# Global attention's value products: hi and lo parts side by side, 5 matmuls in place of 13

## The chip, the cores and the metric

One core of a Trainium2 chip runs the whole program. The metric is device time in microseconds (us) of one execution of the program, the median of several runs. The engines named here are TensorE (PE; PEld is its weight load), VectorE (DVE), ScalarE (ACT), GpSimd (POOL) and SyncE (SP, which issues the DMAs).

## The reference

The program computes attention and, on its output, a two-layer network without gating.

```python
# batch 8, heads 8, 512 local and 32 global positions, head size 64; window 32
k_all = concat([k_g, k_l]);  v_all = concat([v_g, v_l])
out_g = softmax(q_g @ k_all.T / 8) @ v_all                 # 32 global queries see all 544 keys
out_l = softmax([q_l @ k_g.T / 8, banded(q_l @ k_l.T / 8)]) @ concat([v_g, v_l])
x = concat([out_g, out_l]).transpose(0, 2, 1, 3).reshape(8 * 544, 512)
h = maximum(x @ w_in, 0)                                    # w_in 512 x 2048
y = (h * h) @ w_out                                         # w_out 2048 x 512
```

The change lies in the product of `out_g`: probabilities of the global queries times all values.

## The kernel before

**Split numbers.** Most products are made in a rounded fp32 form (F32R). A number is kept as a head (the value rounded to that form, by a copy on ACT) and a rest (value minus head, by a subtraction on DVE), and a product becomes head x head + head x rest + rest x head: three matmuls that add up in one PSUM tile.

**Steps.** A loop over t runs one step for each piece of local attention (16 half sequences of 256 queries, times 8 heads: t = 0 to 127), and in the same step one eighth of a block of the network (step m = t - 9 of it). Within a step PE does, in this order: the transposes of the last piece's probabilities (`pt`), the scores of this piece (`s`), the first layer (`h`, 24 matmuls in two halves), the last piece's value product (`xa`), a part of the global scores (`gs`), and the second layer for the network's step before (`o`, 12 matmuls). ACT and DVE prepare what these need: the row maximum (DVE; CUSTOM_DVE_ANT_0 in the profile, ISA in the lists below), `exp` (ACT, `prob`), the heads `ph` (four ACT copies) and rests (`pl`, `ph`) of the probabilities, the relu `r` of `h` and its square (on ACT in the steps where t mod 16 is in `SQ`, 2, 3, 4, 5, 14 or 15, else on DVE), the head `x_h` and rest `x_l` of the attention output, and in `split_head(t + 1)` the head `hi` (ACT) and rests `lo` and `hi` (DVE) of the queries, keys and values of the next piece, which the next step's scores read.

**Order.** From t = 17 on, PE, DVE and ACT issue their instructions in the order of the code (`FREE`, `keep_in_program_order`); before that a scheduler may reorder them. An instruction that waits holds back all that is behind it on its engine. In a step, the head and rest of the network's `r` (`act2`: `gh` on ACT, `gl` on DVE) come ahead of the jobs of place 1, the last of the step.

**Global attention.** Four heads of a batch (a group) form one global softmax; there are 16 such groups, and each needs two value products, one per pair of heads (`g_av`, pair 0 and pair 1). The jobs of a group are hung into steps by the table at line 654: with d mod 16 = 11 or 1, the probabilities are transposed at the end of step d + 2 (`g_tr`), their rests are made in step d + 3 (`g_rest`), `g_av` of pair 0 stands at the very end of step d + 3 (t mod 16 = 14 or 4), and `g_av` of pair 1 at the end of step d + 6 (t mod 16 = 1 or 7). One step later `g_x` transposes the result `gxs` into `xg` (DVE). `g_av` (line 333) makes 13 matmuls with 64 weight columns and 128 moving columns into one tile `gxo`: for each of four chunks of keys head x head, head x rest and rest x head, and one more for the last 32 keys, whose head and rest already share their partitions. Then ACT scales `gxo` by the reciprocal of the softmax's sum into `gxs`. `gxo` shares its PSUM buffer with `xa` (tag "xa").

**Output.** In every step with t mod 8 = 2, `evac` copies two finished tiles of the network's output to SBUF (ACT, `ot`).

Of the kernel before, what the change touches and what calls it, by code (L numbers as in the profile page):

```python
# [7 lines left out]
F32 = mybir.dt.float32  # L8
F32R = mybir.dt.float32r
I32 = mybir.dt.int32  # L10
AF = mybir.ActivationFunctionType
# [5 lines left out]
P = 128  # L17
# [20 lines left out]
def f(ap):  # L38
    return ap.bitcast(F32)
# [19 lines left out]
def attention_moe(  # L59
# [10 lines left out]
    pe, ve, ac = InOrder(tc, nc.tensor), InOrder(tc, nc.vector), InOrder(tc, nc.scalar)  # L70
# [3 lines left out]
    p2 = ctx.enter_context(tc.tile_pool(name="p2", bufs=2))  # L74
    p1 = ctx.enter_context(tc.tile_pool(name="p1", bufs=1))
    ps_h = ctx.enter_context(tc.tile_pool(name="ps_h", bufs=2, space=PSUM))
    ps_o = ctx.enter_context(tc.tile_pool(name="ps_o", bufs=1, space=PSUM))
    ps_a = ctx.enter_context(tc.tile_pool(name="ps_a", bufs=1, space=PSUM))
# [3 lines left out]
    def plain(t):  # L82
        return t < NPLAIN
# [179 lines left out]
    state = {}  # L263

    def g_load(t):

        b, grp = t // 16, (t // 4) % 2

        def cols(z, j):
            return bass.AP(z.tensor, z.offset + 64 * j, [list(z.ap[0]), [256, 2], [160, 2], [1, 32]])  # L270

        src = qg[b, grp].rearrange("p (a b) n -> p a b n", a=2)
        if plain(t):
            qz = p1.tile([P, 512], F32, tag=("ph", "gvl", "gvh", "ph")[t // 4], name=f"qz{t}")
            nc.gpsimd.memset(qz, 0.0)
            qr = p1.tile([P, 2, 2, 32], F32, tag="qr", name=f"qr{t}")
            (nc.sync if t else nc.scalar).dma_start(qr, src)
            nc.gpsimd.tensor_copy(cols(qz, 0), qr)
        else:
            qz = qgz  # L280
            qr = p1.tile([P, 2, 2, 32], F32, tag="qr", name=f"qr{t}")
            nc.sync.dma_start(qr, src)
            ac.copy(cols(qgz, 0), qr)
            ve.tensor_sub(cols(qgz, 1), qr, f(cols(qgz, 0)))
        state["qz"] = qz
# [32 lines left out]
    def g_split_v(t, pair):  # L318

        gv = state["gv"]  # L320
        gvh = p1.tile([P, 5, P], F32R, tag="gvh", name=f"gvh{t}_{pair}")
        gvl = p1.tile([P, 4, P], F32R, tag="gvl", name=f"gvl{t}_{pair}")
        ac.copy(gvh, gv)
        ve.tensor_sub(gvl, gv[:, :4, :], f(gvh[:, :4, :]))
        ve.tensor_sub(gvh[32:64, 4, :], gv[32:64, 4, :], f(gvh[32:64, 4, :]))
        state["gvs"] = gvh, gvl

    def g_soft(t):
        s = sg[:, (t // 4) % 2, :]
# [17 lines left out]
    def g_tr(t):  # L347

        s = sg[:, (t // 4) % 2, :]
        gt = ps_a.tile([P, 512], F32, tag="xa", name=f"gt{t}")  # L350
        for c in range(4):
            pe.transpose(gt[:, 128 * c : 128 * c + 128], s[:, 128 * c : 128 * c + 128], ident)
        pth = p1.tile([P, 640], F32R, tag="pth", name=f"pth{t}")
        ac.copy(pth[:, :512], gt)
        state["gpt"] = pth, gt

    def g_tr_last(t):

# [4 lines left out]
        state["ge"] = ge  # L363

    def g_rest(t):
        (pth, gt), ge = state["gpt"], state["ge"]
        ptl = p1.tile([P, 512], F32R, tag="ptl", name=f"ptl{t}")
        ac.copy(pth[:64, 512:], ge[:64, :])
        ve.tensor_sub(ptl, gt, f(pth[:, :512]))
        ve.tensor_sub(pth[64:, 512:], ge[64:, :], f(pth[:64, 512:]))  # L370
        state["gpt"] = pth, ptl

    def g_av(t, pair):
        (gvh, gvl), (pth, ptl) = state["gvs"], state["gpt"]
        xo = ps_a.tile([64, P], F32, tag="xa", name=f"gxo{t}_{pair}")
        mm = []
        for c in range(4):
            cols = slice(128 * c + 64 * pair, 128 * c + 64 * pair + 64)
            mm += [(pth[:, cols], gvh[:, c, :]), (pth[:, cols], gvl[:, c, :]), (ptl[:, cols], gvh[:, c, :])]
        mm.append((pth[:, 512 + 64 * pair : 576 + 64 * pair], gvh[:, 4, :]))  # L380
        for i, (x, y) in enumerate(mm):
            pe.matmul(xo, x, y, start=i == 0, stop=i == len(mm) - 1)
        xs = p1.tile([64, P], F32, tag="xs", name=f"gxs{t}_{pair}")
        ac.activation(out=xs, in_=xo, func=AF.Copy, scale=state["gst", t][:64, pair : pair + 1])
        state["xs"] = xs

    def g_x(t, pair):
# [114 lines left out]

    def evac(blk, tiles=(0, 1)):
        for i in tiles:
            pool, tag = ((p1, "ot"), (p2, "gl"))[i]
            ot = pool.tile([P, DM], F32, tag=tag, name=f"ot{blk}_{i}")
            ac.copy(ot, moe["o"][i])
            if blk < NGR:
                b, hf = divmod(blk, 2)
                r0 = b * 544 + 32 + hf * 256 + i * P  # L510
                nc.sync.dma_start(out[r0 : r0 + P, :], ot)
            else:
                for bb in range(4):
                    r0 = (4 * i + bb) * 544
                    nc.sync.dma_start(out[r0 : r0 + 32, :], ot[32 * bb : 32 * bb + 32, :])
# [59 lines left out]
    def w_done(m):  # L575
        w_used.update(range(4 * m, 4 * m + 4))
        for i in (4 * m, 4 * m + 2):
            w_free(i)

    g_load(0)  # L580
    for t in range(4, 8):
        load_head(t)
# [6 lines left out]
    for t in range(NSTEP + LAG + 1):  # L589
# [29 lines left out]
        if 0 < m <= NSTEP and m % 8 == 1 and m > 8:  # L619
            evac(m // 8 - 1)  # L620
# [24 lines left out]
        if live:  # L645
            if t % 2 == 1:
                g_evac(t)
            if t % 4 == 3 and t + 1 < NT:
                g_load(t + 1)
        elif t == NT:  # L650
            state["gs"] = None
        if live and t % 4 == 3 and (t // 8) % 2 == 1:
            d = t if t % 8 == 3 else t + 2
            for at, *job in (
                (d, 2, g_load_v, 0),
                (d + 1, 3, g_soft),
                (d + 1, 1, g_exp),
                (d + 2, 3, g_norm),
                (d + 2, 1, g_tr),
                (d + 3, 5, g_tr_last),  # L660
                (d + 3, 4, g_rest),
                (d + 3, 3, g_split_v, 0),
                (d + 3, 2, g_load_v, 1),
                (d + 3, 1, g_av, 0),
                (max(d + 4, 17), 3, g_x, 0),
                (d + 5, 2, g_split_v, 1),
                (max(d + 6, 17), 1, g_av, 1),
                (max(d + 7, 18), 3, g_x, 1),
            ):
                place, job, *args = job  # L670
                jobs.setdefault((at, place), []).append((job, t, *args))
        for job, *args in jobs.pop((t, 2), ()):
            job(*args)
        if m == NSTEP:
            for i in range(2):
                gemm2(m - 1, 0, (i,))
                gemm2(m - 1, 1, (i,))
                evac(NBLK - 1, (i,))
        elif m > 0:
            gemm2(m - 1, 0)  # L680
# [12 lines left out]
        if 8 * NGR - 2 <= m < 8 * NGR:  # L693
            cols = (slice(0, 224), slice(224, HALF))[m % 2]
# [76 lines left out]
```

## Time and profile before

| | |
|---|---|
| median of three runs | 1068.76 us (1068.66 to 1069.08) |
| the profiled execution | 1068.82 us, span 1067.0 us |
| granted TensorE clock | 1.0 throughout |
| busy | PE 98%, PEld 88%, DVE 80%, ACT 71% |
| matmuls | 7568, of them 416 of `g_av` |
| `g_av` | 32 of them, ACT's scaling 364 ns each |

In the timelines a row gives the start, the duration, the engine, the line, the operation, output<-inputs with the shape, how many rows are merged, and in brackets how long the engine sat idle before it and what it waited for. Line 52 is the helper that records every operation, so the tile names tell the place. Matmul durations overlap: the distance between two starts is what a matmul takes from the engine. A step of PE lasts from one `pt` to the next. The profiled execution ran 1.8 us beyond its span.

### The profile page before, as it was taken

To read this page: it belongs to the slowest core of one execution; us is meant where nothing else is said; L and a number is where in the kernel's file an instruction comes from. 1 tells how busy PE (TensorE), PEld (TensorE's weight loads), DVE (VectorE), ACT (ScalarE), POOL (GpSimd) and SP (SyncE) were. 2 spreads that over 40 slices of the span, in tenths; PEclk is the share of its full clock that TensorE was granted. 3 is DMA by queue.
4 is the path that set the end of the run, shared out by engine and by line. 5 is a ranking of instruction groups with operands and counts; after the bars stand their busy time and mean duration, and the time that the engine had idled before them with its cause. 6 is when DMAs were issued, how large, how long until landed. Compare 5 with 4: busy or idle time off the path is not lost.

```text
span 1067.0 us, 21142 instructions
## 1 busy us (share of the span) xinstructions
PE 1050.4 (98%) x7568; PEld 941.7 (88%) x7568; DVE 856.3 (80%) x2687; ACT 753.1 (71%) x1901; POOL 3.9 (0%) x14
## 2 busy tenths in 40 slices
PE   7999999999999999999999999999999999999998
PEld 6776889999998989998999989999999989999896
DVE  5698988898888989988888888888888888874321
ACT  5898877778777776778777777777777787774322
POOL 1000000000000000000000000000000000000000
PEclk9999999999999999999999999999999999999999
DMA  9772132223222322222322222223221322201000
GB/s 372 310 263 74 57 106 76 71 80 98 68 89 64 103 65 83 74 91 77 94 71 82 86 72 76 90 66 100 78 89 55 94 86 66 88 29 33 13 20 20
DMA packets 54312, 96.78 MB, mean 91 GB/s; under 512 B 4288, under 2 KB 29376, under 8 KB 54208
## 3 DMA queue, kind: packets, MB, share of 16 engines
q1 hardware_dynamic: 54064, 95.37, 27.2%
q8 instruction: 60, 0.98, 0.4%
q14 instruction: 44, 0.36, 0.1%
q10 hardware_dynamic: 144, 0.07, 0.0%
HBM read 86.51 MB, written 8.91 MB: 89 GB/s over the span
## 4 chain that ended last, share of the span: by engine, by line
PE 87%; ACT 7%; DVE 4%; issue 1%; DMA 0%; ACTq 0%
PE o L52 33%; PE h L52 32%; PE xa L52 7%; PE s L52 6%; PE pt L52 5%; PE gxo L52 2%; PE gs L52 2%; ACT prob L52 1%; DVE prob L52 1%; ACT r L52 1%; ACT ph L52 1%; ACT hi L52 1%; ACT ot L52 1%; PE gt L52 1%; ACT sg L52 0%
## 5 line engine op out<-in xcount | busy, mean ns | idle before, releaser
L52 PE MATMUL h<-x_h,ws 128*128 128x256 f32 x2048 | 388.9, 283 | 0.0
L52 PEld LDWEIGHTS h<-x_h,ws 128*128 128x128 f32 x2048 | 327.0, 191 | 0.5
L52 PE MATMUL o<-ws,gh 128*128 128x512 f32 x1024 | 321.3, 395 | 0.0
L52 PE MATMUL h<-x_l,ws 128*128 128x256 f32 x1024 | 289.1, 282 | 0.1
L52 PEld LDWEIGHTS o<-ws,gh 128*128 128x128 f32 x1024 | 185.5, 188 | 34.6
L52 PE MATMUL o<-ws,gl 128*128 128x512 f32 x512 | 202.6, 396 | 0.0
L52 PEld LDWEIGHTS h<-x_l,ws 128*128 128x128 f32 x1024 | 195.9, 191 | 0.9 <-DVE x_l L52 0.4
L52 ACT CAST ph<-pt 128x256 fp32r<-128x256 f32 x448 | 141.1, 341 | 67.7 <-PE pt L52 60.8
L52 ACT ACTIVATE prob<-prob,st 128x224 f32<-128x224 f32 x270 | 127.8, 475 | 61.2 <-DVE st L52 59.1
L52 ACT ACTIVATE r<-h 128x512 f32<-128x512 f32 x136 | 81.4, 599 | 112.3 <-PE h L52 112.3
L52 PEld LDWEIGHTS o<-ws,gl 128*128 128x128 f32 x512 | 96.2, 188 | 22.7
L52 DVE CUSTOM_DVE_ANT_0 prob<-s,con 128x224 f32<-128x224 f32 x256 | 90.0, 386 | 24.5 <-PE s L52 23.2
L52 DVE TENSOR_TENSOR gl<-r,gh 128x512 fp32r<-128x512 f32 x128 | 87.9, 686 | 23.3 <-ACT gh L52 20.5
L52 ACT CAST hi<-raw 128x864 fp32r<-128x864 f32 x112 | 102.5, 915 | 1.4
L52 DVE TENSOR_TENSOR r<-h,r 128x512 f32<-128x512 f32 x82 | 56.7, 692 | 51.9 <-ACT r L52 50.6
L52 PE MATMUL xa<-ph,hi 128*64 128x128 f32 x448 | 87.3, 238 | 1.6 <-DVE ph L52 1.2
L52 DVE TENSOR_TENSOR hi<-raw,hi 64x352 fp32r<-64x352 f32 x224 | 82.5, 368 | 6.4
L52 ACT CAST gh<-r 128x512 fp32r<-128x512 f32 x128 | 79.1, 618 | 9.1 <-DVE r L52 8.7
L52 DVE TENSOR_TENSOR ph<-pt,ph 64x128 fp32r<-64x128 f32 x224 | 79.6, 355 | 7.0
L52 DVE TENSOR_TENSOR lo<-raw,hi 128x448 fp32r<-128x448 f32 x112 | 69.6, 622 | 15.3 <-ACT hi L52 12.5
L52 PE MATMUL pt<-con,prob 128*128 128x128 f32 (+1 forms) x512 | 78.2, 274 | 0.7 <-ACT prob L52 0.5
L52 DVE TENSOR_SCALAR prob<-prob,st 128x224 f32<-128x224 f32 x242 | 70.7, 334 | 4.1
(80 smaller groups left out, 1572.7 us busy)
## 6 DMA issues: line engine op xcount, KB each, us to landing
raw<-in_pk_dram SPq DMA_DIRECT2D x127, 432.0 KB, 3.2
wr<-in_w_dram SPq DMA_DIRECT2D x32, 512.0 KB, 7.9
gv<-in_vg_dram SPq DMA_DIRECT2D x32, 320.0 KB, 3.3
out_dram<-ot SPq DMA_DIRECT2D x32, 256.0 KB, 2.2
qr<-in_qg_dram SPq DMA_DIRECT2D x31, 64.0 KB, 2.8
out_dram<-ot SPq DMA_DIRECT2D x8, 64.0 KB, 1.7
con<-in_consts_dram SPq DMA_DIRECT2D x2, 224.0 KB, 5.1
raw<-in_pk_dram SPq DMA_DIRECT2D x1, 304.0 KB, 3.2
```

The lines of the kernel that those rows point to most:

```text
L52: r = method(*args, **kwargs)
```

## The change

The heads and rests of the transposed probabilities go into one tile `pts`, interleaved so that 64 columns of heads and the 64 columns of their rests stand side by side for each chunk and pair. The heads and rests of the values go into one tile `gvs` of nine rows. A chunk is then one matmul with 128 weight columns (heads, rests) and 256 moving columns (value heads, value rests), into a PSUM tile of 128 partitions by 2 x 128. Its four quarters are head x head, head x rest, rest x head, and rest x rest, which nobody reads. The last 32 keys stay one small matmul into the first quarter. The three quarters that count are added outside of PE: a copy of the first (ACT), two additions (DVE), and then the scaling (ACT), which now reads SBUF.

Three buffers get other neighbours, since the two tiles are larger: the early tile `qz` of steps 4 to 7 goes from the tag "gvl" to the tag "r", and the first of the two output tiles `ot` from a tag of its own to "pth", the buffer of `pts`.

```diff
     def g_split_v(t, pair):
-        gvh = p1.tile([P, 5, P], F32R, tag="gvh", name=f"gvh{t}_{pair}")
-        gvl = p1.tile([P, 4, P], F32R, tag="gvl", name=f"gvl{t}_{pair}")
+        gvs = p1.tile([P, 9, P], F32R, tag="gvh", name=f"gvh{t}_{pair}")
+        gvh, gvl = gvs[:, :5, :], gvs[:, 5:, :]
         ac.copy(gvh, gv)
         ve.tensor_sub(gvl, gv[:, :4, :], f(gvh[:, :4, :]))
...
     def g_tr(t):
...
-        pth = p1.tile([P, 640], F32R, tag="pth", name=f"pth{t}")
-        ac.copy(pth[:, :512], gt)
+        pts = p1.tile([P, 1152], F32R, tag="pth", name=f"pth{t}")
+        pc = pts[:, :1024].rearrange("p (c h n) -> p c h n", c=8, h=2)
+        gc = gt.rearrange("p (c n) -> p c n", c=8)
+        ac.copy(pc[:, :, 0, :], gc)
...
     def g_rest(t):
-        ac.copy(pth[:64, 512:], ge[:64, :])
-        ve.tensor_sub(ptl, gt, f(pth[:, :512]))
-        ve.tensor_sub(pth[64:, 512:], ge[64:, :], f(pth[:64, 512:]))
+        ac.copy(pts[:64, 1024:], ge[:64, :])
+        ve.tensor_sub(pc[:, :, 1, :], gc, f(pc[:, :, 0, :]))
+        ve.tensor_sub(pts[64:, 1024:], ge[64:, :], f(pts[:64, 1024:]))
     def g_av(t, pair):
-        xo = ps_a.tile([64, P], F32, tag="xa", name=f"gxo{t}_{pair}")
+        xo = ps_a.tile([P, 2, P], F32, tag="xa", name=f"gxo{t}_{pair}")
         mm = []
         for c in range(4):
-            cols = slice(128 * c + 64 * pair, 128 * c + 64 * pair + 64)
-            mm += [(pth[:, cols], gvh[:, c, :]), (pth[:, cols], gvl[:, c, :]), (ptl[:, cols], gvh[:, c, :])]
-        mm.append((pth[:, 512 + 64 * pair : 576 + 64 * pair], gvh[:, 4, :]))
-        for i, (x, y) in enumerate(mm):
-            pe.matmul(xo, x, y, start=i == 0, stop=i == len(mm) - 1)
+            o = 256 * c + 128 * pair
+            mm.append((xo, pts[:, o : o + 128], gvs[:, c : c + 6 : 5, :]))
+        mm.append((xo[:64, 0, :], pts[:, 1024 + 64 * pair : 1088 + 64 * pair], gvs[:, 4, :]))
+        for i, (o, x, y) in enumerate(mm):
+            pe.matmul(o, x, y, start=i == 0, stop=i == len(mm) - 1, skip_group_check=True)
         xs = p1.tile([64, P], F32, tag="xs", name=f"gxs{t}_{pair}")
-        ac.activation(out=xs, in_=xo, func=AF.Copy, scale=state["gst", t][:64, pair : pair + 1])
+        ac.copy(xs, xo[:64, 0, :])
+        ve.tensor_add(xs, xo[:64, 1, :], xs)
+        ve.tensor_add(xs, xo[64:, 0, :], xs)
+        ac.activation(out=xs, in_=xs, func=AF.Copy, scale=state["gst", t][:64, pair : pair + 1])
```

The instructions stand as follows at the `g_av` of pair 0 at the end of step 78 (names carry buffer numbers, which differ between the two kernels). On ACT, the end of step 78 and the start of step 79, before:

```order
L52 CAST gh_7641<-r_7616 128x512 [waits Activation_49]
L52 ACTIVATE gxs_0_7659<-gxo_0_7645,gst_7371 64x128 [waits PE_49]
L52 CAST ph_7685<-pt 128x256 [waits DVE_49,PE_49]
L52 CAST ph_7685<-pt 64x128
L52 CAST ph_7685<-pt 32x256 x2
L52 ACTIVATE prob_94,st_7691<-prob_94,st_7691 128x224 [waits DVE_49]
```

and now:

```order
L52 CAST gh_7535<-r_7510 128x512 [waits Activation_49]
L52 COPY gxs_0_7545<-gxo_0_7539 64x128 [waits PE_49]
L52 ACTIVATE gxs_0_7545<-gxs_0_7545,gst_7267 64x128 [waits DVE_49]
L52 CAST ph_7574<-pt 128x256 [waits PE_49]
L52 CAST ph_7574<-pt 64x128
L52 CAST ph_7574<-pt 32x256 x2
```

ACT used to wait for PE alone here; now its scaling waits for DVE, and the four `ph` copies of the next step stand behind it. On DVE at the same place, before:

```order
L52 TENSOR_TENSOR hi_7621<-raw_7430,hi_7621 64x352 [waits PE_49]
L52 TENSOR_TENSOR hi_7621<-raw_7430,hi_7621 32x64
L52 TENSOR_TENSOR gl_7642<-r_7616,gh_7641 128x512 [waits Activation_49]
L52 ISA prob_94,st_7691<-s_7667,con 128x224 [waits PE_49]
L52 ISA st_7691 128x1
```

and now:

```order
L52 TENSOR_TENSOR hi_7515<-raw_7326,hi_7515 64x352 [waits PE_49]
L52 TENSOR_TENSOR hi_7515<-raw_7326,hi_7515 32x64
L52 TENSOR_TENSOR gl_7536<-r_7510,gh_7535 128x512 [waits Activation_49]
L52 TENSOR_TENSOR gxs_0_7545<-gxo_0_7539,gxs_0_7545 64x128 [waits Activation_49]
L52 TENSOR_TENSOR gxs_0_7545<-gxo_0_7539,gxs_0_7545 64x128 [waits DVE_49]
L52 ISA prob_94,st_7580<-s_7556,con 128x224 [waits PE_49]
```

The two additions stand behind `hi` and `gl` and ahead of the next step's row maximum. All other rows of the steps from 17 on keep their order; in steps 13 to 16, where a scheduler orders them, some neighbours change places.

More of the change, by code (lines that the diff above doesn't have):

```diff
@@ L273, in g_load @@
         if plain(t):
-            qz = p1.tile([P, 512], F32, tag=("ph", "gvl", "gvh", "ph")[t // 4], name=f"qz{t}")
+            qz = p1.tile([P, 512], F32, tag=("ph", "r", "gvh", "ph")[t // 4], name=f"qz{t}")
             nc.gpsimd.memset(qz, 0.0)
@@ L325, in g_split_v @@
         ve.tensor_sub(gvh[32:64, 4, :], gv[32:64, 4, :], f(gvh[32:64, 4, :]))
-        state["gvs"] = gvh, gvl
+        state["gvs"] = gvs
     def g_soft(t):
@@ L352, in g_tr @@
             pe.transpose(gt[:, 128 * c : 128 * c + 128], s[:, 128 * c : 128 * c + 128], ident)
-        pth = p1.tile([P, 640], F32R, tag="pth", name=f"pth{t}")
-        ac.copy(pth[:, :512], gt)
-        state["gpt"] = pth, gt
+        pts = p1.tile([P, 1152], F32R, tag="pth", name=f"pth{t}")
+        pc = pts[:, :1024].rearrange("p (c h n) -> p c h n", c=8, h=2)
+        gc = gt.rearrange("p (c n) -> p c n", c=8)
+        ac.copy(pc[:, :, 0, :], gc)
+        state["gpt"] = pts, pc, gc
     def g_tr_last(t):
@@ L365, in g_rest @@
     def g_rest(t):
-        (pth, gt), ge = state["gpt"], state["ge"]
-        ptl = p1.tile([P, 512], F32R, tag="ptl", name=f"ptl{t}")
-        ac.copy(pth[:64, 512:], ge[:64, :])
-        ve.tensor_sub(ptl, gt, f(pth[:, :512]))
-        ve.tensor_sub(pth[64:, 512:], ge[64:, :], f(pth[:64, 512:]))
-        state["gpt"] = pth, ptl
+        (pts, pc, gc), ge = state["gpt"], state["ge"]
+        ac.copy(pts[:64, 1024:], ge[:64, :])
+        ve.tensor_sub(pc[:, :, 1, :], gc, f(pc[:, :, 0, :]))
+        ve.tensor_sub(pts[64:, 1024:], ge[64:, :], f(pts[:64, 1024:]))
     def g_av(t, pair):
-        (gvh, gvl), (pth, ptl) = state["gvs"], state["gpt"]
-        xo = ps_a.tile([64, P], F32, tag="xa", name=f"gxo{t}_{pair}")
+        gvs, pts = state["gvs"], state["gpt"][0]
+        xo = ps_a.tile([P, 2, P], F32, tag="xa", name=f"gxo{t}_{pair}")
         mm = []
         for c in range(4):
-            cols = slice(128 * c + 64 * pair, 128 * c + 64 * pair + 64)
-            mm += [(pth[:, cols], gvh[:, c, :]), (pth[:, cols], gvl[:, c, :]), (ptl[:, cols], gvh[:, c, :])]
-        mm.append((pth[:, 512 + 64 * pair : 576 + 64 * pair], gvh[:, 4, :]))
-        for i, (x, y) in enumerate(mm):
-            pe.matmul(xo, x, y, start=i == 0, stop=i == len(mm) - 1)
+            o = 256 * c + 128 * pair
[3 more added lines that the diff above has]
+            pe.matmul(o, x, y, start=i == 0, stop=i == len(mm) - 1, skip_group_check=True)
         xs = p1.tile([64, P], F32, tag="xs", name=f"gxs{t}_{pair}")
-        ac.activation(out=xs, in_=xo, func=AF.Copy, scale=state["gst", t][:64, pair : pair + 1])
+        ac.copy(xs, xo[:64, 0, :])
+        ve.tensor_add(xs, xo[:64, 1, :], xs)
+        ve.tensor_add(xs, xo[64:, 0, :], xs)
+        ac.activation(out=xs, in_=xs, func=AF.Copy, scale=state["gst", t][:64, pair : pair + 1])
         state["xs"] = xs
@@ L504, in evac @@
         for i in tiles:
-            pool, tag = ((p1, "ot"), (p2, "gl"))[i]
+            pool, tag = ((p1, "pth"), (p2, "gl"))[i]
             ot = pool.tile([P, DM], F32, tag=tag, name=f"ot{blk}_{i}")
```

## The prediction

> **What bounds the kernel now.** First the page's busy line and its chain of waits:
>
> ```profile
> PE 1050.4 (98%) x7568; PEld 941.7 (88%) x7568; DVE 856.3 (80%) x2687; ACT 753.1 (71%) x1901; POOL 3.9 (0%) x14
> PE 87%; ACT 7%; DVE 4%; issue 1%; DMA 0%; ACTq 0%
> ```
>
> TensorE sets the end, but 11% of the chain runs over ACT and DVE. Where that happens is seen in the timeline of PE, at the end of step 78 (a `g_av` of pair 0), in step 79 and in steps 80 and 81:
>
> ```profile
> 583.17 0.22 PE L52 MATMUL gxo<-gvh,pth 128*64 128x128 f32 x1
> ...
> 583.95 0.62 PE L52 MATMUL pt<-con,prob 128*128 128x128 f32 x4
> ...
> 584.90 0.29 PE L52 MATMUL h<-x_h,ws 128*128 128x256 f32 x1
> ...
> 587.78 0.22 PE L52 MATMUL xa<-ph,hi 128*64 128x128 f32 x1
> ...
> 591.31 0.60 PE L52 MATMUL pt<-con,prob 128*128 128x128 f32 x4
> 591.73 0.34 PE L52 MATMUL s<-hi 128*128 128x224 f32 x1
> ...
> 598.64 0.60 PE L52 MATMUL pt<-con,prob 128*128 128x128 f32 x4
> 598.99 0.35 PE L52 MATMUL s<-hi 128*128 128x224 f32 x1
> ```
>
> The 13 products take 583.95 - 583.17 = 0.78 us, 60 ns each. Without a wait the scores start 0.35 us after `pt` (step 81); in step 80 it is 0.42. What they wait for is the split of the next piece, shown by ACT and then DVE in step 79:
>
> ```profile
> 584.15 0.36 ACT L52 ACTIVATE gxs<-gxo,gst 64x128 f32<-64x128 f32 x1 [0.60 <-PE gxo L52]
> 584.61 1.29 ACT L52 CAST ph<-pt 128x256 fp32r<-128x256 f32 x4
> 586.07 0.48 ACT L52 ACTIVATE prob<-prob,st 128x224 f32<-128x224 f32 x1 [0.17 <-DVE st L52]
> ...
> 588.04 0.60 ACT L52 ACTIVATE r<-h 128x512 f32<-128x512 f32 x1 [0.93 <-PE h L52]
> ```
>
> ```profile
> 584.51 0.69 DVE L52 TENSOR_TENSOR gl<-r,gh 128x512 fp32r<-128x512 f32 x1
> ...
> 590.40 0.63 DVE L52 TENSOR_TENSOR lo<-raw,hi 128x448 fp32r<-128x448 f32 x1 [0.40 <-ACT hi L52]
> 591.06 0.77 DVE L52 TENSOR_TENSOR hi<-raw,hi 64x352 fp32r<-64x352 f32 x2
> ```
>
> ACT waits for `h`, makes `r`, its square, `x_h` and `hi`; DVE waits 0.40 for that `hi`, and PE starts the scores 591.73 - 591.06 = 0.67 us after DVE began the `hi` rest. So PE -> ACT -> DVE -> PE is a loop, 3.69 us from `r` to `s`, that is already closed in this step: PE leads by nothing. The only slack ahead of it on ACT is the bracketed idle time, 0.17 + 0.93 us.
>
> **The change part by part.** *Products.* The new product has the shape of `h` (128 weight columns, 256 moving): 24 of these take 587.78 - 584.90 = 2.88 us, 0.12 each. Four and one small one are 4 x 0.12 + 0.06 = 0.54 us, 0.24 less than 0.78; 32 `g_av` give 7.7 us where PE alone decides.
>
> The Trainium skill ("TensorE: Matmul & The Clock Gate", "What overlaps and what doesn't") lets a weight load overlap running matmuls only in other row groups, which would add the loads of 128 columns to each product, an estimate of 4 x (107 + 109) + 109 = 970 ns against 13 x (53 + 56) = 1420 by its formulas: 14 us saved in all. The rows above with 0.12 us a product do not agree with it, and the sum goes by them.
>
> *The additions.* Prices from the groups (busy us, mean ns) of the nearest shapes, ACT copies and DVE additions of 64 partitions from PSUM:
>
> ```profile
> L52 ACT COPY sg<-gs 64x160 f32<-64x160 f32 x32 | 9.2, 288 | 1.6 <-PE gs L52 0.7
> L52 ACT COPY sg<-gs 64x96 f32<-64x96 f32 x32 | 7.5, 234 | 0.0
> L52 DVE TENSOR_TENSOR sg<-gs,sg 64x160 f32<-64x160 f32 x28 | 8.9, 317 | 0.8
> L52 DVE TENSOR_TENSOR sg<-gs,sg 64x96 f32<-64x96 f32 x28 | 6.7, 239 | 0.0
> L52 DVE TENSOR_TENSOR pth<-gs,pth 64x128 fp32r<-64x128 f32 x16 | 4.7, 294 | 7.1 <-ACT pth L52 7.0
> L52 DVE TENSOR_TENSOR qgz<-qr,qgz 128x128 fp32r<-128x128 f32 x28 | 8.2, 292 | 0.8
> ```
>
> The copy is 0.26 us (between 0.234 and 0.288), an addition 0.28 (0.239 to 0.317). The scaling stays at 0.26 to 0.36. Small as they are, their place counts: the additions stand behind `gl` on DVE, and ACT's scaling, with all of the next step behind it, waits for them. I take 0.03 us between dependent instructions, as from ACT's `hi` to `lo`.
>
> *Case A, pair 0* (t mod 16 = 14 or 4), by the rows above. `gl` ends at 584.51 + 0.69 = 585.20, long after the product (583.17 + 0.48 + 0.22 = 583.87) and its copy (584.17). Additions end at 585.51 and 585.82; the scaling starts at 585.85 and `ph` at 586.17, not 584.61: 1.56 late. ACT's idle 0.17 + 0.93 takes 1.10 of it up, so `r` starts 0.46 late; by the row pair below, where nothing waits (1.34 from `ph` to `exp`, 1.06 from there to the next), it starts at 586.17 + 2.40 = 588.57, 0.53 late. I take 0.50. `s` follows 3.69 after, so PE loses 0.50 us against before, its 0.24 included. The late `ph` also moves `pl` and `ph` on DVE near their use in `xa`; a wait of PE there would fall into the time in which it must wait for `s` anyway. Bounds 0.25 (cheaper prices, no 0.03) and 0.70.
>
> *Case B, pair 1 ahead of an `evac`* (t mod 16 = 1). ACT, DVE and PE around step 82:
>
> ```profile
> 606.89 0.36 ACT L52 ACTIVATE gxs<-gxo,gst 64x128 f32<-64x128 f32 x1 [1.58 <-PE gxo L52]
> 607.40 1.29 ACT L52 CAST ph<-pt 128x256 fp32r<-128x256 f32 x4
> 608.74 0.48 ACT L52 ACTIVATE prob<-prob,st 128x224 f32<-128x224 f32 x1
> ...
> 609.80 1.07 ACT L52 COPY ot<-o 128x512 f32<-128x512 f32 x2
> 610.76 0.62 ACT L52 ACTIVATE r<-h 128x512 f32<-128x512 f32 x1
> ```
>
> ```profile
> 606.31 0.67 DVE L52 TENSOR_TENSOR gl<-r,gh 128x512 fp32r<-128x512 f32 x1
> ...
> 614.06 0.77 DVE L52 TENSOR_TENSOR hi<-raw,hi 64x352 fp32r<-64x352 f32 x2
> ```
>
> ```profile
> 613.97 0.60 PE L52 MATMUL pt<-con,prob 128*128 128x128 f32 x4
> 614.73 0.34 PE L52 MATMUL s<-hi 128*128 128x224 f32 x1 [0.16 <-ACT sg L52]
> ```
>
> From `ph` on ACT waits for nothing (no brackets); the scores start again 0.67 us after `hi`, and 0.76 after `pt`, so this step is ACT's already. `gl` ends at 606.98, the additions at 607.29 and 607.60, the scaling runs from 607.63, and `ph` starts at 607.94 for 607.40: 0.54 late, all of it lost. Bounds 0.35 and 0.75.
>
> *Case C, pair 1 elsewhere* (t mod 16 = 7), DVE and PE in step 88:
>
> ```profile
> 653.32 0.68 DVE L52 TENSOR_TENSOR gl<-r,gh 128x512 fp32r<-128x512 f32 x1
> 654.55 0.39 DVE L52 CUSTOM_DVE_ANT_0 prob<-s,con 128x224 f32<-128x224 f32 x1 [0.55 <-PE s L52]
> ...
> 660.46 0.77 DVE L52 TENSOR_TENSOR hi<-raw,hi 64x352 fp32r<-64x352 f32 x2
> ```
>
> ```profile
> 660.74 0.60 PE L52 MATMUL pt<-con,prob 128*128 128x128 f32 x4
> 661.13 0.34 PE L52 MATMUL s<-hi 128*128 128x224 f32 x1
> ```
>
> The additions fill DVE's idle 0.55 (654.00 to 654.62). The row maximum starts 0.07 late, DVE carries that on to `hi`, and `s` comes 0.67 after it: 0.07 us lost, bounds -0.15 and 0.25.
>
> *The rest.* In the last steps nothing but the network runs; PE is full:
>
> ```profile
> 960.00:1060.00 100.00, 99.92 (x661) 89.93 (x660) 31.29 (x63) 31.31 (x56) 0.00 (x0) 1.00 0.05 18
> ```
>
> Four `g_av` have no next split behind them (t = 126, 129, 132, 135). Three gain 0.24; of the last, the longer path to `xg` ahead of the last block loses about what PE gains: -0.7 in all. The first (t = 14), among instructions that a scheduler moved, I put at 0, between -0.5 and +1.6. The interleaved writes cost nothing: `qgz`, written in short pieces, takes 292 ns for 128 columns as `pth` in one piece takes 294. `ot` in the buffer of `pts` costs nothing: it is filled in steps with t mod 8 = 2, after pair 1 was read, and refilled over a step later. What is written in pieces now:
>
> ```profile
> L52 DVE TENSOR_TENSOR ptl<-gt,pth 128x512 fp32r<-128x512 f32 x16 | 11.0, 687 | 2.2 <-ACT pth L52 1.4
> L52 ACT CAST pth<-gt 128x512 fp32r<-128x512 f32 x16 | 9.4, 587 | 11.7 <-PE gt L52 11.7
> ```
>
> *Sum.* Case A: 13 `g_av` (7 with t mod 16 = 4, 6 with 14) x 0.50 = 6.5. B: 7 x 0.54 = 3.8. C: 7 x 0.07 = 0.5. Rest: -0.7. Together +10.1 us on the profiled execution's 1068.82, which is 0.06 over the median: **1079 us**. The bounds give 3.3 + 2.5 - 1.1 - 1.2 = +3.5 and 9.1 + 5.3 + 1.8 + 0.9 = +17.1.
>
> **The rivals.** *PE alone counts* (the other side): if the scaling held ACT up by no more than its idle time in case A (1.10 less the 0.24 by which PE comes earlier), every `g_av` of A gains 0.24; with B and C at nought or better the time is 1066, and 1061 if all 32 gain. It turns at a `ph` start of 585.47 in step 79, 0.70 earlier than reckoned. For it speaks PE's 98%; against it that the additions alone end at 585.82, since `gl` ends at 585.20, later than both kernels' products. *The delay is taken up later*: were `r` late but `hi` not needed at once, the PE gain and the loss would about cancel, 1067 to 1071. Against it stands the 0.67 us, the same in steps 80, 83 and 89. *Interleaving is dear*: if the writes into `pts` took twice as long (an ACT copy and a DVE subtraction of 0.59 and 0.69 us in each group), steps 13 and 14, or 3 and 4, of 14 groups would lose up to 1.28 us more, 18 us, 1097. Against it only the `qgz` row speaks. *The change saves nothing on PE*, 13 products' worth of time in five: that moves A, B and C little, since `gl` and not the product comes last in them; about 1080.
>
> **How the numbers follow.** My forecast, with the last rival: 0.80. PE alone counts 0.10, the delay taken up 0.05, interleaving 0.05. A change under 0.2% (2.1 us) is about what a measurement of this kernel can't tell from none. Faster by more: 0.09; within it: 0.06; slower: 0.85. The range is 1071 to 1086: the bounds of the sum are 1072 and 1086, and the low end takes in part of the delay taken up.
>
> **What would show it.** `gxo` in 5 matmuls over 0.54 us. ACT's wait of `gxs` for DVE: 1.6 us in A, 0.7 in B, 1.0 in C, some 35 us in all. In step 79 `r` on ACT without a wait for `h`, and 1.1 to 1.2 us between `pt` and `s` of step 80 (0.42 + 0.24 + 0.50); in step 83 1.5 (0.76 + 0.24 + 0.54), in step 89 0.7. Steps without a `g_av` before them keep their length. It is wrong if ACT's idle time before `r` in step 79 stays, or if the additions run ahead of `gl`.

## The result and the profile after

| | median | range, runs | against before in the same session |
|---|---|---|---|
| before | 1068.77 us | 1068.66 to 1069.08, 4 | |
| changed kernel | 1082.35 us | 1082.18 to 1083.10, 4 | 1.0128 (1.0112 to 1.0144) |

The changed kernel is slower by 13.6 us; 1079 had been forecast, with 1071 to 1086 as the range. Its profiled execution took 1082.44 us, with a span of 1080.7 against 1067.0 before. The busy line and the chain of waits of the page after:

```profile
PE 1052.7 (97%) x7312; PEld 938.2 (87%) x7312; DVE 873.0 (81%) x2751; ACT 758.8 (70%) x1933; POOL 3.9 (0%) x14
PE 71%; ACT 16%; DVE 10%; issue 3%; DMA 0%; ACTq 0%
```

PE has 256 matmuls fewer. DVE's 64 additions and ACT's 32 copies are new, 18 and 8 us of work. But the part of the chain that runs over ACT and DVE went from 11% to 26%: the time is in waits, not in work. The waits of the changed kernel (waiter <- releaser: us in all, times, the longest):

```profile
ACT gxs L52 <- DVE gxs L52: 35.8, 31, 1.6
...
DVE pl L52 <- ACT ph L52: 21.3, 29, 1.6
```

The first of them did not exist before; the second was there once:

```profile
DVE pl L52 <- ACT ph L52: 1.9, 1, 1.9
```

ACT's 35.8 us of waiting for the additions had been forecast as "some 35". The wait of `pl` had not: DVE, which makes ACT wait, then waits for ACT itself, 29 times. The groups of the operations that were added or reshaped (busy us, mean ns of one | idle before them):

```profile
L52 DVE TENSOR_TENSOR gxs<-gxo,gxs 64x128 f32<-64x128 f32 x64 | 18.2, 285 | 3.9 <-ACT gxs L52 2.8
...
L52 ACT ACTIVATE gxs<-gxs,gst 64x128 f32<-64x128 f32 x32 | 12.9, 402 | 35.8 <-DVE gxs L52 35.8
...
L52 ACT COPY gxs<-gxo 64x128 f32<-64x128 f32 x32 | 8.3, 258 | 25.6 <-PE gxo L52 25.6
...
L52 ACT CAST pth<-gt 128x512 fp32r<-128x512 f32 x16 | 9.4, 586 | 11.7 <-PE gt L52 11.7
...
L52 DVE TENSOR_TENSOR pth<-gt,pth 128x512 fp32r<-128x512 f32 x16 | 11.0, 687 | 2.1 <-ACT pth L52 1.2
```

Copy and addition cost what was assumed (258 and 285 ns for 0.26 and 0.28 us). The scaling takes longer, 402 ns where at most 0.36 us was assumed, but `ph` starts 0.31 us after it (663.34 and 663.65 in step 88 below), for 0.32 in the prediction. The interleaved writes, the last two rows, take 586 and 687 ns as the plain ones did (587 and 687).

**Where the steps grew.** From the start of one step's scores `s` to the next step's is a step's length. Sorted by t mod 16, only the steps around a `g_av` change, and alike in every cycle; all other steps keep their length within a few hundredths of a us (one, step 76, was 0.23 longer before):

| place of `g_av` | step that holds its product | step after it | sum per `g_av` | all of them | forecast |
|---|---|---|---|---|---|
| A, pair 0 (13 times) | -0.01 | +0.43 | +0.42 | +5.4 | +6.5 |
| B, pair 1 before an `evac` (7) | -0.26 | +0.71 | +0.45 (first +1.2) | +3.9 | +3.8 |
| C, pair 1 elsewhere (7) | -0.26 | +0.94 | +0.68 | +4.7 | +0.5 |
| rest | | | | -0.4 | -0.7 |

Together +13.6, for the 13.7 between the two spans. One sort of place, C, came out 4.2 us above the forecast; A came out 1.1 below it, and B as forecast. Step 88 follows a `g_av` of C. First before, PE, ACT and DVE in order of time:

```profile
653.83 0.35 PE L52 MATMUL s<-hi 128*128 128x224 f32 x1
...
654.17 1.30 ACT L52 CAST ph<-pt 128x256 fp32r<-128x256 f32 x4
...
655.50 0.42 DVE L52 TENSOR_TENSOR pl<-pt,ph 128x256 fp32r<-128x256 f32 x1
```

and the same step in the timeline after:

```profile
662.36 0.35 PE L52 MATMUL s<-hi 128*128 128x224 f32 x1
...
662.70 0.60 DVE L52 TENSOR_TENSOR gxs<-gxo,gxs 64x128 f32<-64x128 f32 x2
663.34 0.39 DVE L52 CUSTOM_DVE_ANT_0 prob<-s,con 128x224 f32<-128x224 f32 x1
663.34 0.40 ACT L52 ACTIVATE gxs<-gxs,gst 64x128 f32<-64x128 f32 x1 [0.88 <-DVE gxs L52]
663.65 1.27 ACT L52 CAST ph<-pt 128x256 fp32r<-128x256 f32 x4
...
664.96 0.42 DVE L52 TENSOR_TENSOR pl<-pt,ph 128x256 fp32r<-128x256 f32 x1 [0.70 <-ACT ph L52]
...
669.38 0.60 PE L52 MATMUL pt<-con,prob 128*128 128x128 f32 x4
669.92 0.77 DVE L52 TENSOR_TENSOR hi<-raw,hi 64x352 fp32r<-64x352 f32 x2
...
670.59 0.34 PE L52 MATMUL s<-hi 128*128 128x224 f32 x1 [0.61 <-ACT ph L52]
```

The row maximum (`prob<-s`) starts 0.98 us after the scores, 0.72 before; that is the small shift of the forecast. But `pl` starts 2.60 after the scores, 1.67 before. In both kernels it starts where ACT's four `ph` copies have ended (655.47 and 664.92), and these begin after the scaling, which waits for the additions. From `pl` to the next scores it is 5.63 us in both kernels (655.50 to 661.13, 664.96 to 670.59): DVE is full from there on, and everything by which `pl` is late arrives at PE. The bracket at PE's `s` names ACT's `ph`, which begins 0.5 us ahead of it; what PE needs of the next piece, `hi`, comes from DVE 0.67 before.

### The profile page after: what moved, and what is told of

It is laid out like the page before. It is cut to its first block, busy times and chain, and to the rows that moved or that the text cites. A ratio compares the mean times of both kernels' runs of the same rounds, so it can differ in the third digit from the quotient of the medians.

```text
span 1080.7 us, 20770 instructions
## 1 busy us (share of the span) xinstructions
PE 1052.7 (97%) x7312; PEld 938.2 (87%) x7312; DVE 873.0 (81%) x2751; ACT 758.8 (70%) x1933; POOL 3.9 (0%) x14
## 4 chain that ended last, share of the span: by engine, by line
PE 71%; ACT 16%; DVE 10%; issue 3%; DMA 0%; ACTq 0%
PE o L52 28%; PE h L52 27%; PE xa L52 5%; PE s L52 4%; ACT ph L52 4%; PE pt L52 3%; ACT r L52 3%; ACT prob L52 2%; ACT hi L52 2%; PE gs L52 2%; DVE hi L52 2%; DVE gl L52 1%; DVE lo L52 1%; DVE prob L52 1%; DVE gxs L52 1%
## 5 line engine op out<-in xcount | busy, mean ns | idle before, releaser
L52 PE MATMUL xa<-ph,hi 128*64 128x128 f32 x448 | 91.0, 240 | 3.9 <-DVE ph L52 3.6
L52 PE MATMUL s<-hi 128*128 128x224 f32 x224 | 63.9, 311 | 11.2 <-ACT sg L52 4.7
```

Of the source, the lines that this page charges most:

```text
L52: r = method(*args, **kwargs)
```

## The experiments

Runs 1 to 4 were timed in one session and runs 5 to 7 in another, each with the kernel before beside them (1068.66 and 1069.0 us). Given for each run are the median, the range, the ratio to the kernel before with its 95% interval, and the change per `g_av` in A, B and C, as in the table above (medians). The theory to be tested: the change costs time because DVE's additions stand between ACT's copy and ACT's scaling, and the late scaling moves `ph` and with it `r` (A), ACT's whole step (B) or DVE's `pl` (C). The rivals: the work added on DVE or ACT fills them up whatever its place; the additions wait too long behind `gl`; or the new product itself costs what was thought to be saved.

**1. The products alone.** The kernel scales the first quarter straight out of PSUM, without copy and additions.

```diff
-        ac.copy(xs, xo[:64, 0, :])
-        ve.tensor_add(xs, xo[:64, 1, :], xs)
-        ve.tensor_add(xs, xo[64:, 0, :], xs)
-        ac.activation(out=xs, in_=xs, func=AF.Copy, scale=...)
+        ac.activation(out=xs, in_=xo[:64, 0, :], func=AF.Copy, scale=...)
```

> The changed kernel without the copy and the two additions: ACT scales the first quarter straight from PSUM, as before the change. It leaves out head x rest and rest x head of the value products. Theory (the way out of PSUM costs, not the product): all 32 products gain 0.24 us, 1061 us (1059.5 to 1063). Rival 1 (five products take as long as thirteen): 1068 to 1069. Rival 2 (the interleaved writes or the new buffers cost): above 1070.

1063.15 us (1062.91 to 1063.52), 0.995 of before (0.9935 to 0.9964), a little above the expected range. The five products do save time, 5.5 us: 0.26 for each `g_av` in B and C, but nothing in A, where 0.24 had been counted each time. So copy and additions cost the other 1082.35 - 1063.15 = 19.2 us, on 26.5 us of new work (18.2 + 8.3 in the groups above), and the new product itself costs nothing, nor do the interleaved writes and the moved buffers, which this run keeps.

**2. The additions alone.** The 13 products of before, and behind them a copy, an addition and a subtraction of the same sizes and in the same places.

```diff
-        ac.activation(out=xs, in_=xo, func=AF.Copy, scale=...)
+        ac.copy(xs, xo)
+        ve.tensor_add(xs, xo, xs)
+        ve.tensor_sub(xs, xs, xo)
+        ac.activation(out=xs, in_=xs, func=AF.Copy, scale=...)
```

> The kernel before with its 13 products, but with the new way out: a copy, two DVE operations of the shape of the additions (plus the product, minus the product, so that the value stays), and the scaling from SBUF. Theory: the products' 0.24 us are worth nothing, since DVE's gl comes after both kernels' products in cases A and C; only case B (0.2 us later, 7 times) and the last steps add to it: 1083 to 1086 us. Rival (products, interleaving or buffers bring the loss): 1068 to 1072.

1086.18 us (1085.90 to 1086.29), 1.0164 (1.0149 to 1.0180), just above the expected range. A +0.41, B +0.68 and C +0.71 per `g_av`. With the additions in, the shorter product is worth 1086.18 - 1082.35 = 3.8 us: 0.23 in each B, next to nothing in A and C, where DVE and not PE sets when the scaling can start, and 1.7 us in the steps up to 16 and after step 126. Taken alone the saving was 5.5 us, so most of the small gain stayed, though partly in other places, and the loss lies on top of it.

**3. The scaling off ACT.** DVE scales, one step later and ahead of the transposes that need it; ACT waits for nothing new.

```diff
         ve.tensor_add(xs, xo[64:, 0, :], xs)
-        ac.activation(out=xs, in_=xs, func=AF.Copy, scale=...)
...
     def g_x(t):
+        ve.tensor_scalar(out=xs, in0=xs, scalar1=..., scalar2=None, op0=ALU.mult)
```

> The changed kernel with the copy and the additions where they are, but the scaling not on ACT: DVE scales a step later, just ahead of the transposes into xg. ACT then waits for DVE nowhere here. Theory (ACT's wait is the cost): case A -0.07, B -0.18, C +0.2 us each against before, 1067 us (1065 to 1070). Rival (DVE's own added work is the cost): 1082 to 1087, as DVE has still more to do.

1068.42 us (1068.16 to 1068.79, ten runs), 0.9998 (0.9988 to 1.0007). A 0.00, B -0.21, C +0.20; the first A and the first B, in steps 20 and 17, stand apart with +0.27 and +0.84. DVE has more work than in the changed kernel (880.7 us busy for 873.0), and 13.9 us are gone, so it is not the amount of work on DVE. Step 88 in its timeline, ACT, DVE and PE in order of time:

```profile
653.53 0.35 PE L52 MATMUL s<-hi 128*128 128x224 f32 x1
...
653.87 1.29 ACT L52 CAST ph<-pt 128x256 fp32r<-128x256 f32 x4 [0.23 <-PE pt L52]
653.89 0.61 DVE L52 TENSOR_TENSOR gxs<-gxo,gxs 64x128 f32<-64x128 f32 x2
655.35 0.42 DVE L52 TENSOR_TENSOR pl<-pt,ph 128x256 fp32r<-128x256 f32 x1
...
656.57 0.28 DVE L52 TENSOR_SCALAR gxs<-gxs,gst 64x128 f32<-64x128 f32 x1
...
661.29 0.34 PE L52 MATMUL s<-hi 128*128 128x224 f32 x1 [0.24 <-DVE hi L52]
```

ACT makes `ph` while DVE still adds. `pl` starts 1.82 after the scores (653.53) and not 2.60, and from it to the next scores it is 5.94: the 5.63 of before and the 0.28 of the scaling with its gap. So C's +0.20 is DVE's own added work on its full path, +0.46, less the product's 0.26.

**4. The same in C alone.** ACT scales as in the changed kernel, but in the seven `g_av` of C, and an eighth in the last steps, DVE does it as in run 3.

```diff
-        ac.activation(out=xs, in_=xs, func=AF.Copy, scale=...)
+        if t_av(t, pair) % 16 != 7:
+            ac.activation(out=xs, in_=xs, func=AF.Copy, scale=...)
...
     def g_x(t):
+        if t_av(t, pair) % 16 == 7:
+            ve.tensor_scalar(out=xs, in0=xs, scalar1=..., scalar2=None, op0=ALU.mult)
```

> As e3, but only for the seven products of case C (t mod 16 = 7), and the eighth in the last steps. Theory (in case C, ph is late by ACT's wait, DVE's pl waits for all four ph copies and idles 0.7 us, and DVE is full from there to hi): case C falls from 0.68 to about 0.2, 1079 us (1078 to 1080). Rival (in case C the additions' 0.6 us on DVE are the loss): C stays at 0.68 or grows by 0.2, 1082 to 1084.

1078.82 us (1078.69 to 1078.97), 1.0096 (1.0079 to 1.0113). C +0.20, A and B unchanged at +0.43 and +0.45. The seven places of C give back 3.5 us and nothing else moves: they are independent of the others.

**5. Copy on ACT, all sums on GpSimd.** ACT copies the four quarters to SBUF in one piece; GpSimd, which is nearly idle (3.9 us busy in the changed kernel), adds and scales.

```diff
-        ac.copy(xs, xo[:64, 0, :])
-        ve.tensor_add(xs, xo[:64, 1, :], xs)
-        ve.tensor_add(xs, xo[64:, 0, :], xs)
-        ac.activation(out=xs, in_=xs, func=AF.Copy, scale=...)
+        ac.copy(xq, xo)
+        nc.gpsimd.tensor_copy(xt, xq[64:, 0, :])
+        nc.gpsimd.tensor_add(xs, xq[:64, 0, :], xq[:64, 1, :])
+        nc.gpsimd.tensor_add(xs, xs, xt)
+        nc.gpsimd.tensor_scalar(out=xs, in0=xs, scalar1=..., scalar2=None, op0=ALU.mult)
```

> The changed kernel with another way out of PSUM: ACT copies all four quarters at once, and GpSimd, which is idle, makes the two additions (after a copy that brings the third quarter to the first partitions) and the scaling in SBUF, ahead of the transposes a step later. ACT and DVE then have no more work than before the change and wait for nothing new. Theory: cases B and C gain the product's 0.26 us as in e1, case A nothing (the scores after the product wait for hi anyway), 1063 us (1062.5 to 1065). Rival (GpSimd is late for the transposes, or slows DVE at SBUF): DVE waits ahead of xg, 1068 or more.

1064.88 us (1064.49 to 1065.08), 0.9963 (0.9948 to 0.9977) of before's 1069.0: this version beats both kernels. A -0.01, B -0.18, C -0.27. It does all of the change's work, within 1.7 us of run 1, which leaves the sums out (1.4 if each is set against the kernel before of its own session). GpSimd's groups:

```profile
L393 POOL TENSOR_SCALAR gxs<-gxs,gst 64x128 f32<-64x128 f32 x32 | 20.0, 624 | 3.1
L391 POOL TENSOR_TENSOR gxs<-gxq 64x128 f32<-64x128 f32 x32 | 19.2, 601 | 2.6
L392 POOL TENSOR_TENSOR gxs<-gxs,gxt 64x128 f32<-64x128 f32 x32 | 15.7, 490 | 2.5
L390 POOL COPY gxt<-gxq 64x128 f32<-64x128 f32 x32 | 10.0, 311 | 893.5 <-ACT gxq L52 893.5
```

The four operations take 311 + 601 + 490 + 624 ns = 2.0 us, against two additions of 285 and a scaling of 402 (1.0 us) in the changed kernel. Twice the time, but almost nothing waits for it: the transposes of `gxs` stand some 3 us behind the copy on DVE, and waited for GpSimd in only three `g_av`, 7.5 us, all in the last steps.

**6. The same copy, all sums on DVE one step later.** As in run 5 ACT is free at once, but the two additions and the scaling stand on DVE ahead of the transposes.

```diff
-        ac.copy(xs, xo[:64, 0, :])
-        ve.tensor_add(xs, xo[:64, 1, :], xs)
-        ve.tensor_add(xs, xo[64:, 0, :], xs)
-        ac.activation(out=xs, in_=xs, func=AF.Copy, scale=...)
+        ac.copy(xq, xo)
...
     def g_x(t):
+        ve.tensor_add(xs, xq[:64, 0, :], xq[:64, 1, :])
+        ve.tensor_add(xs, xq[64:, 0, :], xs)
+        ve.tensor_scalar(out=xs, in0=xs, scalar1=..., scalar2=None, op0=ALU.mult)
```

> As e5, but DVE makes additions and scaling, right ahead of the transposes of the next step instead of right after gl. ACT is as free as in e5. Theory: some 0.95 us more of DVE there; case A takes it up in DVE's idle 0.55 + 0.40 (0 to +0.1), B loses about 0.37 and C about 0.7, where DVE is full up to hi: 1076 us (1073 to 1078). Rival (only ACT's wait costs, DVE's work is covered): 1063 to 1066.

1076.08 us (1075.46 to 1077.54), 1.0069 (1.0054 to 1.0084). A 0.00, B +0.39, C +0.69. Step 88 in its timeline, from PE's scores over DVE's `pl` to the next scores:

```profile
658.58 0.35 PE L52 MATMUL s<-hi 128*128 128x224 f32 x1
...
660.25 0.43 DVE L52 TENSOR_TENSOR pl<-pt,ph 128x256 fp32r<-128x256 f32 x1
...
666.82 0.34 PE L52 MATMUL s<-hi 128*128 128x224 f32 x1 [0.72 <-ACT ph L52]
```

`pl` starts 1.67 after the scores (658.58) as before the change, and from it to the next scores it is 6.57, 5.63 and three operations of 0.28 with their gaps. In C this costs what the late `pl` cost in the changed kernel: DVE's path can be lengthened by a late start or by work put into it. In A the same 0.94 us on DVE cost nothing, since DVE waits for ACT further on in that step: before, 0.55 us at `x_l` (row in the next section) and 0.40 at `lo` (in the prediction's rows), 0.95 in all. It just fits, and in run 6 DVE's step 79 has no idle time left.

**7. The additions ahead of `gl`.** From step 23 on, DVE's `gl` stands behind the jobs of place 1, not ahead of them.

```diff
-            act2(m)
+            rest = act2(m, t >= 23)
...
             job(*args)
+        if run and t >= 23:
+            rest()
```

> The changed kernel, with DVE's gl of the same step moved behind the two additions (from step 23 on); ACT and PE keep their order. Theory: in case A the scaling starts 0.6 to 0.7 us earlier and the loss of 0.43 goes; B stays at 0.46, as the product ends there after hi; C falls from 0.68 to about 0.4: 1075 us (1073 to 1077). Rival (the additions' length, not their place, costs): 1081 to 1083.

1075.44 us (1075.05 to 1076.04), 1.0062 (1.0047 to 1.0077). A 0.00 (without the first, which lies ahead of step 23), B +0.46, C +0.47. In A, where `gl` was in front, the scaling comes 0.6 us earlier and the whole loss is gone. In C it comes 0.2 earlier and so does `pl`, to 2.40 after the scores. In B nothing moves: the additions started right behind ACT's copy already (in step 82 the copy ends at 614.55 + 0.26 = 614.81, and they start at 614.84), and with `gl` out of the way DVE waits for that copy 0.57 us.

**The seven runs side by side**, for steps 82 and 88, each number the distance of two starts in the timelines:

| kernel | step 82: `s` to `ph` (ACT) | `ph` to next `s` | step 88: `s` to `pl` (DVE) | `pl` to next `s` |
|---|---|---|---|---|
| before | 0.33 | 7.33 | 1.67 | 5.63 |
| changed | 1.08 | 7.30 | 2.60 | 5.63 |
| 1, no additions | 0.34 | 7.32 | 1.66 | 5.63 |
| 2, 13 products | 1.05 | 7.29 | 2.36 | 5.63 |
| 3, scaling on DVE | 0.33 | 7.38 | 1.82 | 5.94 |
| 4, the same in C | 1.09 | 7.28 | 1.82 | 5.94 |
| 5, GpSimd | 0.34 | 7.41 | 1.66 | 5.62 |
| 6, sums later | 0.34 | 7.98 | 1.67 | 6.57 |
| 7, ahead of `gl` | 1.08 | 7.30 | 2.40 | 5.62 |

In B the kernels differ in when ACT starts `ph`, in C in when DVE starts `pl`; what follows has one length unless an experiment put work into it. The two columns of a step account for its whole length, so the cause is settled for B and C. For A see the next section.

## Why the prediction was right or wrong

**The bound and the direction** were right: the loop over ACT and DVE was closed, and a wait of 1.6, 0.7 or 0.9 us of ACT for DVE (forecast 1.6, 0.7, 1.0) outweighed what PE saved. The rival "PE alone counts" gave 1061 if all 32 gain; run 1 shows that even without any additions only 1063 is to be had. "Interleaving is dear" fell with the 586 and 687 ns. "The change saves nothing on PE" fell with run 1 and with the five products of step 78, 590.63 to 591.18 below: 0.55 us for 0.54 forecast. The rule of the Trainium skill that the prediction set against the rows ("TensorE: Matmul & The Clock Gate", "What overlaps and what doesn't") would have made them 0.97, an estimate from that page's formulas; the trace does not agree with it here.

**Case C was mis-sized**, and that is the miss of 3.4 us: C cost 4.2 more than forecast, and A gave 1.1 of that back. The step that failed reads "The row maximum starts 0.07 late, DVE carries that on to `hi`". The row maximum did shift by no more than that (0.26 relative to scores that come 0.26 earlier). But between it and `hi` DVE has `pl`, and `pl` waits for ACT's four `ph` copies, which the additions had just made late. The prediction had seen this in A ("the late `ph` also moves `pl` and `ph` on DVE") but only for its use in `xa`, and didn't follow it along DVE to `hi`, in A or in C. +0.68 for +0.07, seven times, makes 4.3 us. Step 89 shows it too: 1.21 us between `pt` and `s` (669.38 and 670.59 above) where 0.7 was forecast. That even the upper bound of 0.25 was passed shows that it was a wait left out, not a price: with the additions priced right, `ph` at 663.65 and its 1.27 us put `pl` at 664.92, 0.93 late relative to the scores, and 0.93 less the product's 0.26 is the measured 0.68. By the code `pl` needs only the first of the four copies, but in step 88 of all nine kernels it starts at the end of the fourth or later. Why, no run shows. ACT and DVE both read the PSUM tile `pt` there; the Trainium skill says ("PSUM — Partial Sum Buffer", "PSUM bank collisions raise a hardware error") that two engines may not access one bank and quadrant at once, and that a compiler's scheduler therefore orders such instructions, reads included; that would fit.

**Case A** was nearly right in size, 0.42 for 0.50, but not in its path, so the size is in part luck. Step 79 of the changed kernel in the timelines of PE, DVE and ACT:

```profile
590.63 0.71 PE L52 MATMUL gxo<-gvh,pth 128*128 128x256 f32 x5
...
591.18 0.61 PE L52 MATMUL pt<-con,prob 128*128 128x128 f32 x4
591.18 0.77 DVE L52 TENSOR_TENSOR hi<-raw,hi 64x352 fp32r<-64x352 f32 x2
...
591.85 0.34 PE L52 MATMUL s<-hi 128*128 128x224 f32 x1
...
594.84 0.42 DVE L52 TENSOR_TENSOR pl<-pt,ph 128x256 fp32r<-128x256 f32 x1 [0.70 <-ACT ph L52]
...
595.90 0.60 ACT L52 ACTIVATE r<-h 128x512 f32<-128x512 f32 x1
...
596.19 0.30 PE L52 MATMUL xa<-ph,hi 128*64 128x256 f32 x1 [0.15 <-DVE ph L52]
...
597.32 0.92 ACT L52 CAST hi<-raw 128x864 fp32r<-128x864 f32 x1
...
597.98 0.42 DVE L52 TENSOR_TENSOR x_l<-xa,x_h 64x256 fp32r<-64x256 f32 x1
598.32 0.61 DVE L52 TENSOR_TENSOR lo<-raw,hi 128x448 fp32r<-128x448 f32 x1
...
599.26 0.60 PE L52 MATMUL pt<-con,prob 128*128 128x128 f32 x4
599.62 0.35 PE L52 MATMUL s<-hi 128*128 128x224 f32 x1
```

and three rows of the same step before, of PE and DVE:

```profile
584.38 0.34 PE L52 MATMUL s<-hi 128*128 128x224 f32 x1
...
585.94 0.42 DVE L52 TENSOR_TENSOR pl<-pt,ph 128x256 fp32r<-128x256 f32 x1
...
589.59 0.42 DVE L52 TENSOR_TENSOR x_l<-xa,x_h 64x256 fp32r<-64x256 f32 x1 [0.55 <-ACT x_h L52]
```

`r` has no bracket: ACT's idle time before it is used up, as forecast. It starts 4.05 after the scores, 0.39 later than before (588.04 - 584.38 = 3.66). But ACT no longer sets `hi` on DVE. Where DVE's `lo` waits for ACT's `hi`, it starts 0.03 after its end, as in this step before (590.37 and 590.40); now it starts 0.08 after it (598.24 and 598.32), in all 13 `g_av` of A, and without a bracket. What sets it is DVE itself. `pl` is 1.43 late relative to the scores (2.99 after them, 1.56 before), and from there to the next scores it is 4.78 us and no longer 5.79, since the idle 0.55 and 0.40 of DVE are used up (the rest of the 1.01 is a few hundredths by which the rows of `x_l` and `lo` now overlap). 1.43 - 1.01 = 0.42 is the whole loss. So the late `pl`, left out in C, ends last in A as well; DVE's idle time hides most of it here. The path over `r` alone would have cost about 0.05 less (an estimate from the 0.08 and 0.03).

PE arrives at the same moment by a way of its own. Between `pt` and `s` of step 80 stand 0.36 us and not the 1.1 to 1.2 of the forecast, so PE no longer waits there. It has waited in two places earlier. One is `s` of step 79 itself: 0.67 after `pt` (0.43 before), because it waits for step 78's own `hi`, 591.18 + 0.67 = 591.85; PE's 0.24 from the shorter product is lost right there, and run 1 shows that it was never to be had in A. The other is `xa`, which waits for DVE's rests of `ph`, behind `pl`: its last product starts 4.34 after the scores, 3.87 before. The late `ph` thus reaches PE over DVE's `hi` and over `xa` at once (a wait at `xa` falls into the wait for `s`, as the prediction said), and since every run that removed one delay removed the other too, these runs don't tell which of the two would set the end alone.

**Case B** was right in place and size: `ph` 0.75 late relative to the scores (0.54 + 0.24 forecast), +0.45 for +0.54 net, 1.39 us between `pt` and `s` of step 83 for 1.5. In step 82 ACT's scaling and DVE's row maximum both follow the additions:

```profile
614.55 0.26 ACT L52 COPY gxs<-gxo 64x128 f32<-64x128 f32 x1 [1.34 <-PE gxo L52]
...
614.84 0.61 DVE L52 TENSOR_TENSOR gxs<-gxo,gxs 64x128 f32<-64x128 f32 x2
...
615.49 0.40 ACT L52 ACTIVATE gxs<-gxs,gst 64x128 f32<-64x128 f32 x1 [0.68 <-DVE gxs L52]
615.79 1.27 ACT L52 CAST ph<-pt 128x256 fp32r<-128x256 f32 x4
...
621.70 0.60 PE L52 MATMUL pt<-con,prob 128*128 128x128 f32 x4
...
623.09 0.34 PE L52 MATMUL s<-hi 128*128 128x224 f32 x1 [0.79 <-ACT sg L52]
```

Only the first B, in step 17, cost 1.2 in place of 0.5. Run 3, in which ACT does not wait for the additions, leaves 0.84 of it, run 6, with all sums on DVE and ACT free, has 1.44, and runs 1 and 5, without additions on DVE, have none; so there most of it is DVE's added work and not ACT's wait.

**The rest** came to -0.4 for -0.7: the steps up to 16 gained 0.5, where nothing had been counted, step 76 gave 0.2 that have no part in the change (runs 1 to 7 all have it), and the last steps lost 0.2, where a gain of 0.7 had been counted.

## What to carry to other kernels

On engines that run in order, a small operation is priced by what stands behind it and by every wait that crosses from one engine to the other: 0.6 us of additions in a wait between ACT and DVE cost 19 us in all, and the same sums on an idle engine, twice as slow, cost 1.7. When a delay on one engine has been followed to the end, go through the other engines' next instructions once more and ask which of them waits for the delayed one; do that in each place for itself, since the engine that ends last is not the same everywhere. And a saving on the busiest engine counts only in steps where that engine does not wait right after it: 0.26 us in B and C, none in A.

## What the runs showed of the hardware beyond that

Two operations that share no data slow each other. In run 5 GpSimd's first addition of 64x128 took 0.78 or 0.79 us in the 14 `g_av` in which DVE's `gl` ran beside it, and 0.45 or 0.46 in all others but one early one (0.52); `gl`, a subtraction of two SBUF tiles, took 0.71 to 0.74 in these 14, and 0.67 to 0.69 elsewhere and before. Steps 79 and 82 in its timeline, GpSimd and DVE:

```profile
581.51 0.72 DVE L52 TENSOR_TENSOR gl<-r,gh 128x512 fp32r<-128x512 f32 x1
581.77 0.78 POOL L391 TENSOR_TENSOR gxs<-gxq 64x128 f32<-64x128 f32 x1
...
603.29 0.67 DVE L52 TENSOR_TENSOR gl<-r,gh 128x512 fp32r<-128x512 f32 x1
...
604.50 0.46 POOL L391 TENSOR_TENSOR gxs<-gxq 64x128 f32<-64x128 f32 x1
```

GpSimd's scaling ran beside DVE's `pl` and `ph`, one input of which lies in PSUM, and took 0.60 there (but for one early one), as in the last steps, where nothing ran on DVE beside it. The second addition took 0.45 or 0.46 but for two, of 0.79 and 1.28, and these two ran beside DVE operations with two SBUF inputs again. The Trainium skill states such contention for DVE instructions with two SBUF inputs ("GPSIMD Engine Reference", "1. Specifications"); the rows agree. In step 82, a B, a DVE operation of two elements a row (`st`) took 0.25 us beside GpSimd and 0.17 in run 1, and ACT's `exp`, which waits for it, came 0.09 later: that is the 0.09 by which the step after a `g_av` of B is longer in run 5 than in run 1.

The other difference is small: ACT's scaling of 64x128 took 402 ns from SBUF, where it took 364 from PSUM before.
